# A fixed list of some 1,280 steps laid out anew on five engines and the DMA queue

## The chip, the cores and the metric

The program runs on one core of a Trainium2 chip. A core has five engines, each with an instruction list of its own that it works off in order: TensorE (PE in the profile; PEld is its weight load), VectorE (DVE), ScalarE (ACT), GpSimd (POOL) and SyncE (SP), which here only issues transfers. Engines wait for each other through semaphores. The metric is the device time of one execution in microseconds; lower is better.

## The reference, cut to what matters

```python
# q, k, v: (4, 8, 768, 64); chunks of 32 keys, 24 of them
k_min, k_max = min and max of k over each chunk
ub = sum over d of maximum(q * k_min, q * k_max)       # (B, H, S, 24)
ub = where(causal, ub, -1e9)
top_chunks = the 6 chunks with the largest ub, for each query
scores = matmul(q, k.T) / 8, kept where the chunk is selected and causal
attn = softmax(scores)
x = matmul(attn, v), heads side by side               # (3072, 512)
h = x @ moe_w_in                                      # (3072, 2048)
g = maximum(h, 0) + log1p(exp(-abs(h)))               # softplus
return g @ moe_w_out                                  # (3072, 512)
```

## The kernel before

Attention and feed-forward run side by side. Two heads of one batch make a pair, 16 pairs in all. The pairs of batch 0 are split into halves of the sequence (units 0 to 3 and 4 to 7, three tiles of 128 rows each); the pairs of batches 1, 2 and 3 are whole units (8 to 11, 12 to 15, 16 to 19, six tiles). All that any engine does is one list, the string `ORDER` (line 21 on), worked off at build time: each word is a step, and each step puts its instructions at the end of the lists of its engines. So the order of the words is the order on every engine and in SP's queue, and nothing is reordered at run time: what stands behind a waiting instruction on its engine waits too. A last letter V, A or G names the engine of a copy (VectorE, ScalarE, GpSimd). A tile from a pool waits until an earlier tile's last reader is done; the PSUM pools `ps_big`, `ps_sm` and `ps_w` have two buffers each, the float loads three per kind.

The steps, with unit u, head e, batch b, half h:

- `bk`, `bq`, `bv` (line 211): loads of batch 0, 128 KB each, three to a tile; `hk`, `hq`, `hv` (218, 221, 226): their casts to bf16. `Lk`, `Lq`, `Lv` (232): loads of a whole pair, 384 KB; `ck`, `cq`, `cv` (247, 250): their casts; `fk`, `fq` (267): their transposes by DMA. `w0` to `w3` (501, 504): the two weights, 1 MB each step, issued by GpSimd.
- `kt`, `qt` (276, 283): transposes on TensorE (units 0 to 7). `rg` (290): max or min of K over each chunk; `pk` (295): packs them; `kr`, `qr` (299, 303): K and Q into the operand tiles `Kaug`, `Qaug`; `ar` (203): constant rows of Kaug. `qp`, `qn` (311, 316): positive and negative part of Q; `qp` is a max with 0 on VectorE, or a Relu activation on ScalarE.
- `U` (326, 327): the bounds; `Ua`, `M`, `T` (333, 340, 348 and 349): causal mask, the eight largest, and the selection as rows to be added to Q. These rows reach `Qaug` through TensorE and a copy in units 0 to 7 (`a`, `ac`: 357, 362) and 8 to 11 (`s`, `sc`: 368, 372). In units 12 to 19 `cr` (253) casts Q into one of two row buffers `selqs`, `T` writes its rows beside it, and the flip `fs` (258), a DMA transpose on SP for each head, brings both into `Qaug`. `cr` of unit u + 2 writes the buffer of unit u again.
- `S` (407): scores, in three groups a head; `E` (413): exp; `D` (418): the mask of the diagonal blocks, on GpSimd; `V` (434): times values; `n` (444 to 450): normalisation; `X`, `x` (456, 466) or the DMA transpose `fx` (263): into `xT`.
- `I` (476): four matmuls of the first feed-forward product; `P` (480): softplus; `F` (488): two matmuls of the second; `ob` (492): its copy out of PSUM; `O` (496): the store. `tE` and `tP` (181) change ScalarE's table between exp and softplus.

An `I` block of a batch's half needs all four of its pairs; `F` steps fill TensorE between the `S` and `V` of the next batch.

Of the kernel before, what the change touches and what calls it, by code (L numbers as in the profile page):

```python
# [27 lines left out]
bq1.1.0 hv0.0.0.G U2 qn3 bq1.1.1 E0.0.0 a1.0 hv0.0.1.G Ua2 ac1.0.V a1.1 bq1.1.2 D0.1 M2 S1.0.0 bv1.0.0 D0.0 ac1.1.V
V0.1 E1.0.0 T2 bv1.0.1 U3 S1.1.0 Ua3 bv1.0.2 V0.0 D1.0 M3 E1.1.0 a2.0 bv1.1.0 n0 bv1.1.1 D1.1 ac2.0.V a2.1 bv1.1.2 T3
S2.0.0 Lk8 ac2.1.V a3.0 E2.0.0 a3.1 Lq8 ac3.0.V ac3.1.V V1.0 Lv8 D2.0 V1.1 S2.1.0 n1 S3.0.0 E2.1.0 V2.0 X0 E3.0.0  # L30
S3.1.0 D2.1 x0.A V2.1 D3.0 E3.1.0 n2 X1 hk1.0.A x1.V D3.1 X2 V3.0 V3.1 x2.A Lk9 kt4 n3 kt5 z0 kr4.1.A kr4.0.A rg5.0 X3
# [532 lines left out]
```

## Time and profile before

| | |
|---|---|
| median of 3 runs | 275.47 us (274.07 to 276.18) |
| profiled execution, first to last instruction | 271.8 us |
| TensorE busy | 246.8 us (91%) |
| ScalarE busy | 180.2 us (66%) |
| VectorE busy | 123.0 us (45%) |
| GpSimd busy | 109.5 us (40%) |
| feed-forward matmuls, `F` and `I` | 94.8 and 91.8 us |
| scores, `S` | 52.4 us |

The profile shows one execution. Busy shares are means over the whole span; which wait ends last in a stage is read from that stage. The times of the table of runs and the span of the profiled execution differ by 3.7 us.

### The profile page before, as it was taken

To read this page: it belongs to the slowest core of one execution; us is meant where nothing else is said; L and a number is where in the kernel's file an instruction comes from. 1 tells how busy PE (TensorE), PEld (TensorE's weight loads), DVE (VectorE), ACT (ScalarE), POOL (GpSimd) and SP (SyncE) were. 2 spreads that over 40 slices of the span, in tenths; PEclk is the share of its full clock that TensorE was granted. 3 is DMA by queue.
4 is the path that set the end of the run, shared out by engine and by line. 5 is a ranking of instruction groups with operands and counts; after the bars stand their busy time and mean duration, and the time that the engine had idled before them with its cause. 6 is when DMAs were issued, how large, how long until landed. Compare 5 with 4: busy or idle time off the path is not lost.

```text
span 271.8 us, 5937 instructions
## 1 busy us (share of the span) xinstructions
PE 246.8 (91%) x2295; PEld 153.4 (56%) x2328; DVE 123.0 (45%) x451; ACT 180.2 (66%) x240; POOL 109.5 (40%) x177
## 2 busy tenths in 40 slices
...
GB/s 154 222 195 219 212 169 194 189 151 247 191 233 246 199 189 199 224 160 238 198 151 237 167 177 169 136 128 8 31 2 39 70 68 42 39 0 41 77 77 77
DMA packets 119900, 39.19 MB, mean 144 GB/s; under 512 B 113728, under 2 KB 115776, under 8 KB 119872
## 3 DMA queue, kind: packets, MB, share of 16 engines
...
q8 instruction: 18, 0.29, 0.4%
q14 instruction: 10, 0.08, 0.1%
...
## 4 chain that ended last, share of the span: by engine, by line
PE 87%; ACT 5%; DMA 2%; issue 2%; DVE 2%; POOL 1%; SPq 1%; ACTq 0%; DVEq 0%; POOLq 0%
PE hp L476 30%; PE op L488 30%; PE sc L407 15%; PE o_ps L434 8%; ACT Kaug L203 2%; ACT Kaug L299 1%; DMA Qaug<-row 1%; DMA kf<-in_k_dram 1%; PE ub L326 1%; PE ub L327 1%; PE x_ps L456 1%; PE qa L357 1%; ACT attnT L413 1%; ACT kbh L218 1%; PE sT L368 1%
## 5 line engine op out<-in xcount | busy, mean ns | idle before, releaser
L488 PE MATMUL op<-w_out_sb,gT 128*128 128x512 bf16 x351 | 94.8, 382 | 1.5
L413 ACT ACTIVATE attnT<-sc 128x1024 bf16<-128x1024 f32 (+3 forms) x96 | 82.9, 916 | 16.1 <-PE sc L407 15.4
L476 PE MATMUL hp<-xT,w_in_sb 128*128 128x384 bf16 x512 | 91.8, 326 | 0.2
L480 ACT ACTIVATE gT<-hp 128x768 bf16<-128x768 f32 x64 | 49.2, 808 | 47.1 <-PE hp L476 47.0
L476 PEld LDWEIGHTS <-w_in_sb 128*128 128x128 bf16 x512 | 49.6, 98 | 37.2 <-issue 0.5
L407 PE MATMUL sc<-Qaug,Kaug 128*128 128x128 bf16 (+3 forms) x400 | 52.4, 263 | 1.4 <-ACT attnT L413 0.7
L418 POOL TENSOR_SCALAR_AFFINE_SELECT attnT<-attnT 128x768 bf16<-128x768 bf16 (+1 forms) x40 | 29.2, 731 | 57.3 <-ACT attnT L413 56.9
L488 PEld LDWEIGHTS <-gT 128*128 128x128 bf16 x384 | 35.3, 98 | 28.5 <-issue 0.4
L407 PEld LDWEIGHTS <-Kaug 128*128 128x128 bf16 x400 | 30.6, 101 | 20.8 <-issue 3.0
L434 PEld LDWEIGHTS <-attnT 128*128 128x128 bf16 x672 | 25.3, 98 | 3.2 <-POOL attnT L418 0.3
L434 PE MATMUL o_ps<-vaug,attnT 128*128 128x65 bf16 x672 | 26.7, 194 | 0.3 <-DVE Qaug L362 0.2
L492 ACT COPY ob<-op 128x512 f32<-128x512 f32 x21 | 12.3, 584 | 20.9 <-PE op L488 16.9
L299 POOL COPY Kaug<-kT_sb 64x768 bf16<-64x768 bf16 x24 | 20.2, 841 | 13.1 <-issue 7.0
L290 DVE TENSOR_REDUCE km<-kT_sb 128x24 bf16<-128x768 bf16 x24 | 21.9, 941 | 1.8 <-DMA kT_sb<-kb 1.8
L295 POOL COPY kmm<-km 64x48 bf16<-64x48 bf16 (+1 forms) x40 | 10.4, 259 | 15.9 <-DVE km L290 13.8
L340 DVE MAX8 m<-ubm 128x8 f32<-128x8 f32 (+4 forms) x192 | 16.3, 159 | 0.4
L181 ACT ACT_TABLE_LOAD x11 | 14.1, 1283 | 1.0 <-PEq L548 0.8
L333 DVE TENSOR_TENSOR ubm<-ub,causal 128x288 f32<-128x288 f32 (+2 forms) x20 | 7.5, 379 | 14.8 <-PE ub L327 14.8
L450 DVE TENSOR_TENSOR on<-o_ps,rr 128x384 bf16<-128x384 f32 x24 | 13.4, 557 | 0.8
L492 DVE COPY ob<-op 128x512 f32<-128x512 f32 x3 | 2.0, 682 | 24.0 <-PE op L488 24.0
L449 DVE RECIPROCAL rr<-o_ps 128x6 f32<-128x6 f32 x24 | 4.6, 192 | 18.3 <-PE o_ps L434 18.0
L247 POOL CAST kb<-kf 128x768 bf16<-128x768 f32 x12 | 11.2, 930 | 3.4 <-DMA kf<-in_k_dram 3.3
...
## 6 DMA issues: line engine op xcount, KB each, us to landing
...
w_in_sb<-in_moe_w_in_dram POOLq DMA_DIRECT2D x2, 1024.0 KB, 12.9
...
```

The lines of the kernel that those rows point to most:

```text
L181: A.activation(dummy, dummy, fn)
L290: V.tensor_reduce(st["km2"][:, which, :], st["kT"].rearrange("d (c t g) -> d c t g", t=4, g=CH // 4), axis=AX.XY, op=(ALU.max, ALU.min)[wh ...
L299: COPY[eng](Ka(p, e)[D * (1 - e):D * (2 - e), t0 * 128:t1 * 128], st["kT"][e * D:(e + 1) * D, :])
L340: V.max(out=st["m8"][:, t, e, :], in_=st["ubm"][:, t, 0:max(8, 4 * (t0 + t + 1)), e])
L407: PE.matmul(sc[:, o:o + (z - a) * 128], Ka(p, e)[:, tj * 128:(tj + 1) * 128], Qa(p, e)[:, a * 128:z * 128], start=True, stop=True)
L413: A.activation(st["at", e][:, g * 1024:g * 1024 + n], st["sc", e, g][:, 0:n], ACT.Exp, scale=scale)
L418: G.affine_select(out=d, in_=d, compare_op=ALU.is_ge, fill=0.0, base=0, channel_multiplier=-1, pattern=[[0, n], [1, 128]])
L434: PE.matmul(o[:, t, :], st["at", e][:, a:a + 128], va[:, tj, e, :], start=(tj == 0), stop=(tj == t0 + t))
L476: PE.matmul(hps[b, h, s][:, n, 0:HALF], w_in_sb[:, dt, ft * 128:(ft + 1) * 128], xT[b][:, dt, h * HALF:(h + 1) * HALF], start=(dt == 0), s ...
L480: A.activation(gT[b, h][:, 2 * s:2 * s + 2, :], hps.pop((b, h, s))[:, :, 0:HALF], ACT.Softplus)
L488: PE.matmul(held[b, t], g[:, ft, c:c + 128], w_out_sb[:, ft, :], start=(ft == 0), stop=(ft == KFF - 1))
L492: COPY[eng](obs[b, t], held.pop((b, t)))
```

## The change

`ORDER` is replaced. It holds the same steps (one `tE`, the last of the old list, is gone), in another order, and 130 of the steps that may run on several engines run on another one. Two conditions are changed so that the first step of a tile, whichever it is, allocates it. The list is 81 lines long; shown are the beginning of both and the lines with the steps of units 12 to 19 that are spoken of below.

```diff
@@ -19,81 +19,81 @@
-bk0.0.0 bk0.0.1 augb ident bk0.0.2 cau0 bq0.0.0 kmm bq0.0.1 bq0.0.2 augm rm0.V bk0.1.0 hk0.0.A bk0.1.1 vones rm1.V
-ar1.0.A bk0.1.2 kt0 cau1 kt1 bq0.1.0 rg0.1 ar1.1.A rg0.0 bq0.1.1 kr1.0.A hq0.0.G bq0.1.2 kr0.0.A rg1.0 bv0.0.0 kr0.1.A
-pk0.0.G rg1.1 bv0.0.1 pk0.1.G ar2.0.A qt0 pk1.1.G bv0.0.2 qp0.V pk1.0.G hk0.1.A qn0 bv0.1.0 qt1 U0 kr1.1.A bv0.1.1
-qp1.V ar2.1.A Ua0 kt2 hq0.1.G bv0.1.2 qn1 M0 kt3 kr2.0.A bk1.0.0 U1 rg3.0 kr2.1.A bk1.0.1 ar3.0.A T0 bk1.0.2 rg2.0 w1
-a0.1 kr3.1.A bq1.0.0 rg2.1 kr3.0.A w0 bq1.0.1 Ua1 qt2 ar3.1.A ac0.1.V a0.0 rg3.1 bq1.0.2 pk2.1.G ar0.1.A qp2.V bk1.1.0
-qt3 pk2.0.G ac0.0.V hv0.1.1.G qp3.V bk1.1.1 ar0.0.A S0.1.0 M1 hv0.1.0.G bk1.1.2 pk3.0.G qn2 E0.1.0 S0.0.0 pk3.1.G T1
...
-Lq16 fs13.0 F0.5.7 pk14.0.G I1.1.7.1 cq15.V ob0.5.A pk14.1.G fq15 I1.1.0.0 P1.1.7 Lv16 I1.1.0.1 Lk17 qn14 qp14.V
...
-I1.0.0.0 P1.0.2 F1.3.0 cr14.V I1.0.1.0 Lq17 I1.0.0.1 fs14.0 I1.0.1.1 P1.0.0 fs14.1 rg15.1 kr15.0.G F1.3.1 P1.0.1
-I1.0.4.0 kr15.1.G rg15.0 F1.3.2 I1.0.4.1 pk15.0.G cq16.V pk15.1.G I1.0.3.0 P1.0.4 fq16 F1.3.3 cr15.V Lv17 I1.0.3.1
...
-ck17.G I1.0.5.1 fs15.0 P1.0.7 F1.5.0 fk17 P1.0.5 F1.3.5 Lq18 F1.5.1 rg16.1 tE S13.0.2 S12.1.2 F1.3.6 rg16.0 F1.5.2
...
-cr17.V E13.0.1 O1.3 S12.1.0 D12.0 F1.0.1 qn16 E12.1.0 S12.0.1 qp16.V F1.0.2 E12.0.1 D12.1 S12.0.2 U16 F1.0.3 E12.0.2
...
-E13.1.2 D13.0 fk18 F1.0.5 E13.1.1 F1.5.5 Lq19 cr16.V cv17.G S13.1.0 fx12 V13.0 E13.1.0 rg17.0 fs16.0 kr17.1.G S15.1.2
...
+cau0 bk0.0.0 augb bk0.0.1 bk0.0.2 rm1.V augm ar1.0.G ar3.1.A hk0.0.V bq0.0.0 ident vones bq0.0.2 ar0.0.A bk0.1.1
+bq0.0.1 bk0.1.2 kt1 rg1.1 kmm kt0 kr1.0.A kr1.1.A kr0.0.A rm0.G ar0.1.G ar2.1.A bk0.1.0 bq0.1.1 bq0.1.0 hq0.0.G rg0.0
+rg1.0 pk1.1.A hk0.1.G rg0.1 kr0.1.V bv0.0.1 bk1.0.2 qt0 pk0.0.A bq0.1.2 hq0.1.G qt1 pk0.1.V qp0.A qn0 qn1 ar1.1.A U0
+qp1.A kt2 Ua0 M0 pk1.0.A ar2.0.A T0 rg2.1 bk1.0.0 U1 rg2.0 kt3 a0.1 Ua1 kr2.0.V pk2.1.G kr2.1.A pk2.0.A ac0.1.A
+kr3.1.V M1 a0.0 qt2 bk1.1.0 bv0.0.2 bk1.0.1 qn2 qp2.A S0.1.0 ac0.0.A T1 rg3.0 rg3.1 bq1.0.0 bv0.1.2 bv0.0.0 E0.1.0
+bq1.1.1 bv0.1.0 bq1.0.2 U2 qt3 ar3.0.G a1.0 bq1.0.1 Ua2 qn3 kr3.0.V hk1.0.A bv0.1.1 a1.1 qp3.A M2 pk3.0.V S0.0.0
+ac1.1.V ac1.0.V hv0.0.0.A E0.0.0 kt4 kt5 pk3.1.V T2 kr5.1.A U3 z0 D0.1 kr5.0.V hv0.0.1.G Ua3 rg5.1 z1 w0 S1.1.0 rg5.0
+hq1.0.V kr4.0.V M3 cau1 rg4.1 a2.0 a2.1 S1.0.0 kr4.1.A ac2.0.A E1.1.0 D0.0 bk1.1.1 bk1.1.2 pk5.1.V V0.1 T3 ac2.1.V
+V0.0 n0 w1 D1.1 S2.0.0 E1.0.0 a3.0 ac3.0.V X0 qt4 a3.1 S2.1.0 E2.0.0 x0.V D1.0 V1.1 hv0.1.0.V rg4.0 pk4.0.V ac3.1.A
+D2.0 S3.0.0 V2.0 qt5 V1.0 hv0.1.1.V qp5.V n1 E2.1.0 E3.0.0 D2.1 S3.1.0 V2.1 E3.1.0 qn4 D3.0 X1 pk4.1.V pk5.0.G hk1.1.A
+x1.A n2 D3.1 qp4.V qn5 V3.0 V3.1 X2 n3 kt6 x2.V X3 kt7 x3.V U4 I0.0.3.1 I0.0.3.0 Ua4 I0.0.2.0 rg7.0 bq1.1.0 rg6.1 M4
+bq1.1.2 Lk9 w2 rg6.0 U5 tP P0.0.3 I0.0.2.1 T4 kr6.0.V I0.0.0.0 Ua5 bv1.0.2 bv1.0.0 bv1.0.1 rg7.1 P0.0.2 kr6.1.A
+I0.0.0.1 a4.0 pk6.1.G a4.1 I0.0.1.1 I0.0.1.0 P0.0.0 bv1.1.1 kr7.0.A I0.0.4.1 pk7.0.V I0.0.4.0 hq1.1.V P0.0.1 P0.0.4
+I0.0.7.1 I0.0.7.0 I0.0.6.0 ck9.G qt6 kr7.1.V I0.0.6.1 qt7 M5 ac4.1.A bv1.1.0 bv1.1.2 pk6.0.A P0.0.7 qp6.A T5 I0.0.5.0
+qn6 P0.0.6 ac4.0.A U6 I0.0.5.1 a5.1 qp7.A Ua6 S4.1.1 M6 ac5.1.V a5.0 pk7.1.A qn7 P0.0.5 T6 ac5.0.V U7 tE E4.1.1 S4.1.0
+a6.1 E4.1.0 fk9 Lk8 Ua7 a6.0 ac6.1.V ac6.0.V w3 F0.2.0 F0.1.0 D4.1 M7 F0.2.1 T7 S5.1.0 F0.1.1 S5.1.1 E5.1.0 E5.1.1
+F0.1.2 S4.0.1 a7.1 D5.1 a7.0 E4.0.1 hv1.0.1.V ac7.1.V S4.0.0 V5.1 S5.0.1 E4.0.0 ac7.0.V D4.0 E5.0.1 hv1.0.0.V V4.1
+S5.0.0 F0.2.2 S6.0.1 V4.0 E5.0.0 S6.0.0 F0.2.3 E6.0.1 D5.0 S6.1.0 V5.0 hv1.1.0.V n4 E6.0.0 hv1.1.1.G X4 S6.1.1 D6.0
...
+I1.0.7.1 pk14.0.V I1.0.7.0 I1.1.6.0 kr13.0.A fk15 fq15 Ua13 M13 Lv12 T13 fs13.0 fs13.1 U12 qp14.V Ua12 rg15.1 M12
...
+P1.0.3 I1.1.5.1 I1.1.5.0 F1.3.1 S13.1.0 F1.3.2 P1.1.5 qn15 T12 ck16.V fs12.1 tE E13.1.0 Ua14 cr15.V F1.0.1 F1.3.3
+F1.0.2 S12.1.0 F1.0.3 fs12.0 Lq16 D13.1 fk16 E12.1.0 S13.1.1 F1.0.4 F1.3.4 S12.0.0 E13.1.1 F1.3.5 rg15.0 F1.0.5
...
+F1.5.5 S15.1.0 E14.0.1 cv14.G ck19.G ob1.2.V E15.1.0 F1.5.6 n13.0 T16 cr16.G pk17.1.V kr16.1.V Lk18 cr17.G Lv15 O1.3
+fx12 V14.1 fs16.1 S15.0.1 U17 S15.1.1 Ua17 E15.0.1 F1.5.7 F1.4.0 S15.0.2 M17 T17 E15.1.1 E15.0.2 F1.4.1 ob1.5.V V14.0
+S15.0.0 F1.4.2 fs17.1 fs16.0 S15.1.2 cv15.A D15.1 E15.0.0 kr17.0.G F1.4.3 E15.1.2 F1.1.0 n14.0 S16.1.1 fk19 E16.1.1
+n14.1 S16.1.0 E16.1.0 V15.1 F1.4.4 S17.1.0 E17.1.0 Lv17 F1.1.1 D15.0 ck18.V rg19.0 S17.1.2 rg19.1 F1.1.2 V15.0 fx14
...
+I2.1.3.1 I2.1.3.0 O1.5 I2.0.2.1 P2.1.3 D16.1 kr18.0.G O1.2 I2.0.2.0 P2.0.2 ob1.1.A U18 Ua18 M18 D17.0 T18 F2.0.0
...
+S17.0.1 tE E17.0.1 V16.1 F2.2.0 fs18.1 fs18.0 F2.0.3 S18.1.0 F2.0.4 T19 E18.1.0 kr19.1.V kr19.0.V F2.2.1 fs19.0 F2.0.5
...
+S19.0.0 S18.0.0 V18.1 E18.0.0 ob2.0.V E19.0.0 O2.0 fs19.1 F2.1.0 F2.2.6 S18.0.1 F2.1.1 O1.4 E18.0.1 D19.0 n18.1 F2.2.7
...
@@ -204,7 +204,7 @@
     def load0(c, h, g, t):
-        if t == 0:
+        if (c, h, g) not in quad:
@@ -469,7 +469,7 @@
-        if n == 0:
+        if (b, h, s) not in hps:
```

## Rows read from the trace of the kernel before

**Rows 1.** Table of stages, its sum line: us, busy us of each engine

```profile
sum 271.80, PE 246.81 PEld 153.38 DVE 123.00 ACT 180.25 POOL 109.51; mean PE 17.63 PEld 10.96 DVE 8.79 ACT 12.88 POOL 7.82
```

**Rows 2.** Table of stages: stage, busy us of each engine (instructions), granted clock, DMA, GB/s

```profile
27.75:41.48 13.73, 12.90 (x112) 8.15 (x110) 7.29 (x26) 11.01 (x19) 6.97 (x16) 1.00 1.06 190
...
41.48:61.95 20.47, 18.91 (x257) 13.45 (x258) 11.60 (x49) 17.83 (x22) 11.99 (x16) 1.00 1.08 180
...
136.95:150.00 13.05, 8.12 (x108) 5.60 (x108) 6.37 (x25) 5.42 (x7) 5.32 (x7) 0.74 1.07 192
```

**Rows 3.** TensorE in order of time, 26 to 32 us: start, us, work

```profile
27.75 3.00 PE L476 MATMUL hp<-xT,w_in_sb 128*128 128x384 bf16 x16
```

**Rows 4.** Chain that ended last, 128 to 152 us: start, us, what

```profile
137.74 2.90 DMA Qaug<-row
...
141.89 0.22 PE ub L326
```

**Rows 5.** Waits of TensorE and of VectorE: total us, times, longest

```profile
PE ub L326 <- DVE qpos L311: 4.9, 1, 4.9
...
DVE row L253 <- DMA Qaug<-row: 9.0, 1, 9.0
```

**Rows 6.** The same table in steps of 5 us, 140 to 150 us

```profile
140.00:145.00 5.00, 3.11 (x20) 1.57 (x21) 3.10 (x18) 0.71 (x1) 0.62 (x1) 0.50 0.98 184
145.00:150.00 5.00, 4.95 (x88) 4.03 (x88) 3.27 (x7) 3.65 (x5) 4.22 (x6) 0.91 1.21 233
```

**Rows 7.** The same table, from K's landing to the first `I` step

```profile
4.60:27.75 23.15, 15.28 (x178) 11.26 (x179) 16.04 (x70) 19.69 (x31) 12.36 (x27) 1.00 1.13 213
```

**Rows 8.** Groups of instructions by shape: busy us, mean ns, idle us ahead

```profile
L290 DVE TENSOR_REDUCE km<-kT 128x12 bf16<-128x384 bf16 x16 | 8.5, 553 | 4.9 <-PE kT L276 2.2 <-issue 1.8 <-ACT Kaug L299 0.8
...
L362 DVE COPY Qaug<-qa 128x384 bf16<-128x384 bf16 x16 | 5.3, 350 | 0.8 <-PE qa L357 0.6
...
L253 DVE CAST row<-qf 128x768 bf16<-128x768 f32 x6 | 4.9, 818 | 9.1 <-DMA Qaug<-row 9.0
...
L311 DVE TENSOR_SCALAR qpos<-qT 128x384 bf16<-128x384 bf16 x8 | 2.7, 354 | 2.9 <-PE qT L283 2.8
...
L311 DVE TENSOR_SCALAR qpos<-qT_sb 128x768 bf16<-128x768 bf16 x12 | 4.5, 377 | 0.0
...
L299 ACT COPY Kaug<-kT 64x384 bf16<-64x384 bf16 x16 | 7.4, 472 | 0.3
...
L218 ACT CAST kbh<-kf 128x768 bf16<-128x768 f32 x4 | 3.3, 832 | 2.4 <-DMA kf<-in_k_dram 2.4
...
L181 ACT ACT_TABLE_LOAD x11 | 14.1, 1283 | 1.0 <-PEq L548 0.8
```

**Rows 9.** Chain that ended last, 54 to 65 us: transposes, `F`, `I`

```profile
54.55 0.17 PE x_ps L456 x3
...
59.62 1.29 PE op L488 x6
...
61.95 2.60 PE hp L476 x16
```

**Rows 10.** VectorE in order of time, 142 to 145 us: unit 16

```profile
142.59 0.46 DVE L333 TENSOR_TENSOR ubm<-ub,causal 128x288 f32<-128x288 f32 x1 [0.76 <-PE ub L327]
...
144.20 0.45 DVE L349 TENSOR_TENSOR row<-ubm,m 128x288 bf16<-128x288 f32 x1
```

**Rows 11.** Flips to Qaug, issue to landing, 100 to 183 us

```profile
DMA to landing us min/median/max: 2.7/4.2/7.0
```

**Rows 12.** Issue to landing: loads of 128 KB (L211), then transfers to w_in_sb

```profile
DMA to landing us min/median/max: 2.4/3.5/15.3
...
DMA to landing us min/median/max: 10.4/12.9/15.3
```

**Rows 13.** GpSimd in order of time, 10 to 15 us

```profile
11.21 1.66 POOL L501 DMA_DIRECT2D w_in_sb<-in_moe_w_in_dram  x2
...
14.11 0.95 POOL L226 CAST vaug<-vf 128x384 bf16<-128x384 f32 x2 [0.29 <-DMA vf<-in_v_dram]
```

More of the change, by code (lines that the diff above doesn't have):

```diff
@@ L27 @@
-qt3 pk2.0.G ac0.0.V hv0.1.1.G qp3.V bk1.1.1 ar0.0.A S0.1.0 M1 hv0.1.0.G bk1.1.2 pk3.0.G qn2 E0.1.0 S0.0.0 pk3.1.G T1
[L28 to L31, printed above, removed]
```

106 lines of the change are left out of this document (47 added, 59 removed).

## The prediction

> **What bounds the kernel now.** I read a table of the stages first. Its sum: 271.8 us from first to last instruction, TensorE busy for 246.8 of them [rows 1]. The median of the timed runs is 275.47 us; I make the sum against the profiled 271.8 us and carry the difference, 3.7 us, over unchanged. So all that another order of the same steps can win is some 25 us of idle time and what a low clock costs, none of the matmul work itself. The stages show where TensorE idles [rows 2]. Up to 27.75 us there is no feed-forward work; the first `I` step starts there [rows 3]. Up to 61.95 us TensorE is then idle for 0.83 and 1.56 us (stage length less its busy time). From there it is hardly ever idle, except in the stage 136.95 to 150.00: 13.05 us with 8.12 busy, 4.9 us idle.
>
> That one hole I followed with the chain of waits [rows 4] and the wait tables [rows 5]. TensorE stood at `U16` for 4.9 us, because `qp16` was late on VectorE; VectorE had stood for 9.0 us before `cr16.V`, a cast into one of the two row buffers that units 12 to 19 use in turn, which the flips `fs14` still read; the last of them landed at 140.64 us. So an early cast, waiting in VectorE's list for a transfer late in SP's list, held all behind it. The hole has a second cost: behind it the granted clock is 0.50 for 140 to 145 us and 0.91 for the next five [rows 6], that is 1.2 GHz instead of 2.4. 3.11 us of busy time at half speed lose 1.55 us, 4.95 at 0.91 lose 0.45: 2.0 us. The hole is worth 4.9 + 2.0 = 6.9 us.
>
> **The change, part by part.** No step comes or goes but one spare table load after the last `P`, hidden under closing `F` steps. 130 steps have another engine: GpSimd's lettered steps go from 113 to 57, VectorE's from 67 to 105, ScalarE's from 58 to 76.
>
> *The hole: minus 6.9.* `cr16` goes to GpSimd. Of its six `cr` (14 to 19) VectorE keeps one, `cr15`, and takes `cr12`, which has no flip ahead of it. `cr15` must wait for the flips `fs13`, but `S13.1.0`, which needs them too, stands ahead of it in the list. Behind `cr16` on GpSimd now stand `cr17` and the masks `D15` and `D17`, for which `V15` and `V17` on TensorE would wait; I cost that at nothing, as `fs14.0` stands some 7 us of TensorE's work ahead of `cr16`, and at the old 4.9 us if that cover goes. SP has less ahead of the flips: before `fs13.0` its list holds 23 pair loads, 16 other flips and 4 stores, where it held 26, 18 and 5.
>
> *The start: plus 1.9.* Here VectorE carries more. In 4.60 to 27.75 us it was busy for 16.04 us [rows 7]. Before the first `I` the new list adds four `rg` of units 4 and 5 at 0.553, six `kr` at about 0.35, two `qp` and two `qn` at 0.354, the cast `hq1.0` at up to 0.818, `hk0.0` at up to the same, two `hv` of half its size at 0.4, six `pk` of a sixteenth of its elements at 0.1 (my estimate), two `x` at 0.35: 2.2 + 2.1 + 1.4 + 0.8 + 0.8 + 0.8 + 0.6 + 0.7 = 9.4. It gives away four `qp` and four `ac` at 0.35: 2.8 [rows 8]. (`kr` and `x` go by the copy of L362, the nearest row.) So 16.04 + 9.4 - 2.8 = 22.6 us of work for VectorE. It starts once K is loaded, at about 5 us as before: with no wait the first `I` would start at 27.6 us; with VectorE idle for as long as before, 23.15 - 16.04 = 7.1 us, at 34.7. I take 30.5, nearer to the first: an engine with a longer list waits less, and each wait that work now fills is no loss. Of the 2.75 us by which that is later than 27.75, 0.85 is no loss: `kt6`, `kt7`, `qt4`, `qt5` and `U4` are done by then, 0.17 us each, by three transposes of such a step [rows 9]. Net plus 1.9, ends minus 1.0 and plus 6.1. Behind each of these steps on VectorE stand `Ua`, `M`, `T` of the next unit, and TensorE's `a` steps wait for those.
>
> *Behind the start: minus 1.4.* In 27.75 to 61.95 us 2.4 us are idle [rows 2]; the `kt` and `qt` steps of units 4 to 7, on which TensorE waited there, now lie ahead of the first `I` or behind most of the block. One change of ScalarE's table, 1.28 us [rows 8], stays; I leave 1.0. Ends 0 and minus 2.4.
>
> *The late units: plus 2.0.* This is what the new order pays. I counted TensorE's work between `U` and the first `S` of units 12 to 19 (`I` 0.65, `F` 0.43 a step [rows 9]; `V` and `S` likewise). Before it was 14.7 to 37.8 us; after it is 6.6 (unit 17), 7.1 (18), 7.6 (19), 8.2 (12), 9.6 (16) and 12.9 to 15.2 for the rest. In that time VectorE makes `Ua`, `M`, `T`, 142.59 to 144.65, 2.1 us when nothing is queued ahead [rows 10], and the flip lands 4.2 us after its issue in the median, 2.7 to 7.0 [rows 11]. So 6.3 us are needed, 9.1 at worst. With the median nothing waits; with the worst, 2.5 + 2.0 + 1.5 + 0.9 = 6.9 us. Behind a late flip all of TensorE's list waits, and on SP the second head's flip and the `fx`. I take 2.0, nearer to the median since fewer transfers are ahead; ends 0 and 6.9.
>
> *The relus: 0.* Ten `qp` go to ScalarE. On VectorE they cost 0.354 (units 0 to 7) and 0.377; the nearest rows of ScalarE, copies and casts of such length, take 0.472 and 0.832 [rows 8], so 6 x 0.12 + 4 x 0.46 = 2.6 us more. ScalarE's other work in between gets shorter by six `ob`, six `kr` and two `x`, and TensorE's `I` and `S` cover the rest. Without that cover it is 2.6. The Trainium skill, "ScalarE: Activation LUTs", section "Rules for kernel authors", speaks against this move: relu belongs on VectorE, which it calls up to about three times as fast in bf16. The rows agree on the price (0.377 against 0.832); by that rule the sum would be 273.7, which is rival 5.
>
> *The rest: 0.* In 61.95 to 129.60 and after 150.00 the order keeps TensorE fed with `F` between `S` and `V`; the stores move back in SP's list, each still ahead of the copy that needs its buffer; the tail, copy and store, is the same.
>
> Sum: 271.8 - 6.9 + 1.9 - 1.4 + 2.0 = 267.4; carried to the median, 275.5 - 4.4 = **271.1 us**.
>
> **The rivals.**
> 1. *The start eats the gain* (no change). 128 KB loads landed 3.5 us after issue in the median, but up to 15.3 while the two weight transfers ran, which themselves took 12.9 [rows 12]. Those were issued at 11.21; now they stand behind `hv0.0.1` and `z1` on GpSimd. 18 loads had landed by 14.1 [rows 13], some 0.6 us each, so the 25th, the last that `hq1.0.V` needs, lands at about 18 to 19, just when I expect `w0` to start. If `w0` wins, `hq1.0` holds VectorE, and behind it `M3`, `T3`, `n0` to `n3` and so the first `I`. At the upper end of the start, plus 6.1, it gives 271.1 + 4.2 = 275.3. Against it: those loads are all issued before `w0`.
> 2. *The short chains break* (slower). Place: `S12.1.0` and `S17.1.0`. Landing at 7.0 everywhere costs 6.9 where I took 2.0: 276.0. It decides from the point where one wait is long enough for the clock to fall, as the 4.9 us one did: a flip held on SP by a step that is itself late. One such hole of 6.9 us on top gives 282.9. For it: SP runs in order, and landing already varied from 2.7 to 7.0. Against it: fewer loads ahead.
> 3. *Relu needs its own table* (slower). Each load is 1.28 us, two for each `qp` on ScalarE: 20 x 1.28 = 25.7, of which the first four lie on the start: plus 10.2, 281.3 or more. Against it: 11 loads stand in the trace for 11 deliberate switches [rows 8], and copies run under either table with none. The same skill page, section "Table sets: the hidden batching unit", has relu in every set as filler; by that rule this rival falls, but no relu has run here.
> 4. *Nothing is lost at the start or in the chains*: 271.1 - 2.0 - 2.9 = 266.2, if VectorE never waits and every flip lands in the median.
> 5. *The relus lie on the path*: the first four stand ahead of `U0` to `U3` with nothing to cover them, the others in `I` blocks. All ten uncovered: 271.1 + 2.6 = 273.7.
>
> **How the numbers follow.** About 1% is what a measurement of this kernel can tell from no change: 272.7 to 278.2 us are the same. My forecast, with waits between 0 and 3.5 us, covers 267 to 272.7: 0.48. Rival 4 has 0.07, both faster: 0.55. Rival 1 (0.13), rival 2 without a hole (0.08) and rival 5 (0.04) end within 1%: 0.25. Rival 2 with a hole, 0.16, and rival 3, 0.04, are slower: 0.20. The range leaves out the holes beyond 279, rival 3 and a little below 266.5; the likeliest case's own is 267 to 272.7.
>
> **What would show it.** Right: no wait of VectorE on `Qaug<-row` above 2 us, TensorE's clock at full from 100 to 175 us, the first `I` at 29 to 32 us, each of `S12`, `S15`, `S17` waiting under 1.5 us for a flip. Wrong: a first `I` after 33, `hq1.0` waiting on its load for more than 4 us, a clock of 0.5 in any stretch, or table loads above ten.

## The result, and the profile after

The changed kernel takes 276.8 us (median of 20 runs, 275.6 to 278.5), the kernel before 274.0 us on the same chips (20 runs, 272.3 to 276.7). The ratio is 1.010, 95% interval 1.0078 to 1.0122: 1.0% slower. Forecast were 271.1 us and a gain.

The profiled execution of after has a span of 276.8 us and is the longest of its twenty (273.9 to 276.8). In the runs of both kernels the time is the span plus some 1.7 us; the 3.7 us that the prediction carried over were these 1.7 and another 2.0, since its median came of three runs (275.47, where twenty give 274.0) and the profiled execution of before was a short one (271.8 + 1.7 = 273.5). What follows compares the two profiled spans, 276.8 and 271.8; the medians lie 2.8 us apart, not 5.0.

The busy times on the page of after stand against [rows 1]: engine, busy us, share, instructions. VectorE went up by 20.8 us, GpSimd down by 26.5.

```profile
PE 247.8 (90%) x2295; PEld 155.3 (56%) x2328; DVE 143.8 (52%) x489; ACT 188.1 (68%) x256; POOL 83.0 (30%) x121
```

The table of stages in steps of 10 us, first of after, then of before: stage, length, busy us of TensorE, its weight loads, VectorE, ScalarE, GpSimd (instructions), granted clock, DMA share, GB/s.

```profile
20.00:30.00 10.00, 6.55 (x77) 5.94 (x76) 7.20 (x26) 5.17 (x9) 4.62 (x9) 0.67 1.16 202
30.00:40.00 10.00, 8.16 (x80) 5.39 (x78) 8.28 (x30) 5.80 (x9) 3.96 (x8) 0.82 1.18 207
...
90.00:100.00 10.00, 7.94 (x101) 4.99 (x100) 9.81 (x27) 8.12 (x12) 8.13 (x10) 1.00 0.96 173
100.00:110.00 10.00, 9.02 (x127) 6.78 (x130) 9.09 (x20) 7.66 (x9) 4.50 (x5) 1.00 0.75 168
...
140.00:150.00 10.00, 9.95 (x110) 6.18 (x110) 5.86 (x18) 8.81 (x11) 5.14 (x7) 1.00 0.81 166
150.00:160.00 10.00, 8.94 (x105) 5.62 (x106) 8.23 (x28) 7.82 (x11) 5.78 (x8) 1.00 1.13 212
160.00:170.00 10.00, 8.20 (x120) 5.62 (x118) 8.27 (x29) 7.12 (x9) 4.12 (x5) 1.00 0.79 159
```

```profile
90.00:100.00 10.00, 9.89 (x160) 7.75 (x160) 8.99 (x29) 9.47 (x12) 9.70 (x13) 1.00 1.25 187
...
130.00:140.00 10.00, 6.96 (x46) 3.62 (x44) 1.52 (x3) 7.99 (x11) 2.46 (x4) 0.95 1.02 177
140.00:150.00 10.00, 8.06 (x106) 5.60 (x108) 6.37 (x25) 4.35 (x5) 4.84 (x6) 0.71 1.09 209
```

From tables over the whole span comes the account of the two executions. Idle is stage length less TensorE's busy time, from the table above. Slow clock is an estimate: busy time times what the granted clock lacks of 1.00, from the same table in steps of 1 us, since the clock changes within the stages.

| us | idle before | idle after | slow clock before | after |
|---|---|---|---|---|
| 0 to 40 | 13.3 | 17.0 | 0 | 4.4 |
| 40 to 80 | 1.8 | 0.4 | 0 | 0 |
| 80 to 120 | 0.4 | 3.9 | 0 | 0 |
| 120 to 150 | 5.0 | 0.2 | 2.0 | 0 |
| 150 to 180 | 0.3 | 3.2 | 0 | 0 |
| 180 to the end | 4.2 | 4.2 | 0 | 0 |
| sum | 25.0 | 29.0 | 2.0 | 4.4 |

(Each figure is rounded by itself.) So the hole of [rows 2, 4] and its slow clock are gone: 6.8 us. The start took up to 8.1 back, 80 to 120 us 3.5, 150 to 180 us 3.0; 40 to 80 us gave another 1.4. That makes 6.4 us where the spans differ by 5.0, so the slow clock is put too high. The table in steps of 5 us shows why, first of after, then of new_start_only, an experiment below with the same start:

```profile
25.00:30.00 5.00, 4.90 (x56) 4.59 (x54) 3.14 (x9) 3.64 (x6) 2.06 (x4) 0.50 1.12 203
```

```profile
25.00:30.00 5.00, 4.90 (x57) 4.59 (x55) 3.17 (x9) 3.64 (x6) 2.07 (x4) 1.00 1.12 203
```

In after the clock was at its lower level, 1.2 GHz, and TensorE got through the same work in these 5 us; the first `I` comes at 34.68 us, in new_start_only at 34.21. So up to there the slow clock cost some 0.5 us, as far as one execution of each can say, and the 4.4 is an upper end.

Where TensorE waits now, and one wait of ScalarE (waits of after, as in [rows 5]: engine, line, releaser, us in all, times, longest):

```profile
PE kT L276 <- DVE kbh L218: 6.2, 1, 6.2
PE qT L283 <- DVE km L290: 3.0, 1, 3.0
PE o_ps L434 <- DVE Qaug L362: 2.9, 1, 2.9
PE ub L326 <- DVE kmm L295: 2.2, 2, 1.7
PE ub L326 <- DVE qpos L311: 1.5, 1, 1.5
PE sT L368 <- DVE on L450: 1.3, 1, 1.3
...
PE sc L407 <- DMA Qaug<-row: 0.9, 1, 0.9
...
ACT Kaug L299 <- DVE km L290: 5.7, 2, 3.4
```

Of the waits of TensorE shown here all but one end with VectorE. The first, 6.2 us, is for K's landing and cast. Behind it the longest at the start are 3.0 us before the first `qt` and 2.9 before `V0.1`. The PSUM buffer of `V0.1` is that of `a2.1`, and the copy that frees it, `ac2.1.V`, stands in VectorE's list behind `rg` of units 4 and 5, the cast `hq1.0`, `kr4.0` and `M3`, `T3` (VectorE and TensorE of after in order of time):

```profile
20.84 1.01 DVE L290 TENSOR_REDUCE km<-kT 128x12 bf16<-128x384 bf16 x2
21.77 0.55 DVE L221 CAST row<-qf 128x768 bf16<-128x768 f32 x1
...
24.14 0.35 DVE L362 COPY Qaug<-qa 128x384 bf16<-128x384 bf16 x1
...
24.55 0.82 PE L434 MATMUL o_ps<-vaug,attnT 128*128 128x65 bf16 x12 [2.91 <-DVE Qaug L362]
...
34.68 3.27 PE L476 MATMUL hp<-xT,w_in_sb 128*128 128x384 bf16 x12
```

In 85 to 101 us GpSimd holds VectorE up for part of the time. A copy of 64x48 elements to `kmm`, 0.19 us elsewhere, lasts from 92.23 to 93.88, as long as the memset `zs0` of GpSimd beside it, and `U11` waits. Added up over all of VectorE's instructions, the time above the shortest of the same form is 17.6 us in after, 8.8 in before; records of instructions overlap, so less than that was lost. The rows of the moment (the same view, VectorE, GpSimd and TensorE):

```profile
92.23 1.65 DVE L295 COPY kmm<-km 64x48 bf16<-64x48 bf16 x1
...
92.24 1.59 POOL L512 MEMSET row<- 128x1792 bf16 x1
...
94.98 0.20 PE L326 MATMUL ub<-kmm,qpos 128*128 128x48 bf16 x1 [1.49 <-DVE qpos L311]
```

### The profile page after: what moved, and what is told of

It is laid out like the page before. It is cut to its first block, busy times and chain, and to the rows that moved or that the text cites. A ratio compares the mean times of both kernels' runs of the same rounds, so it can differ in the third digit from the quotient of the medians.

```text
span 276.8 us, 5895 instructions
## 1 busy us (share of the span) xinstructions
PE 247.8 (90%) x2295; PEld 155.3 (56%) x2328; DVE 143.8 (52%) x489; ACT 188.1 (68%) x256; POOL 83.0 (30%) x121
## 4 chain that ended last, share of the span: by engine, by line
PE 73%; DVE 10%; SPq 5%; ACT 5%; DMA 4%; issue 2%; ACTq 0%
PE hp L476 29%; PE op L488 24%; PE sc L407 10%; PE o_ps L434 6%; SPq L211 4%; DVE m L340 2%; DMA Qaug<-row 1%; DMA xT<-on 1%; ACT attnT L413 1%; DMA vf<-in_v_dram 1%; PE x_ps L456 1%; ACT L181 1%; DVE kmm L295 1%; DVE km L290 1%; DVE ubm L333 1%
## 5 line engine op out<-in xcount | busy, mean ns | idle before, releaser
L488 PE MATMUL op<-w_out_sb,gT 128*128 128x512 bf16 x351 | 93.2, 379 | 1.5
L476 PE MATMUL hp<-xT,w_in_sb 128*128 128x384 bf16 x512 | 90.4, 329 | 0.3 <-DMA xT<-on 0.3
L480 ACT ACTIVATE gT<-hp 128x768 bf16<-128x768 f32 x64 | 51.9, 810 | 31.4 <-PE hp L476 31.3
L407 PE MATMUL sc<-Qaug,Kaug 128*128 128x128 bf16 (+3 forms) x400 | 53.5, 262 | 2.2 <-DMA Qaug<-row 0.9
L492 DVE COPY ob<-op 128x512 f32<-128x512 f32 x9 | 6.2, 689 | 54.2 <-PE op L488 54.1
L492 ACT COPY ob<-op 128x512 f32<-128x512 f32 x15 | 8.6, 583 | 21.6 <-PE op L488 21.6
L299 POOL COPY Kaug<-kT_sb 64x768 bf16<-64x768 bf16 x12 | 10.4, 868 | 9.5 <-DMA kT_sb<-kb 9.0
L247 DVE CAST qb<-qf 128x768 bf16<-128x768 f32 x4 | 5.7, 1425 | 11.5 <-DMA qf<-in_q_dram 11.5
L326 PE MATMUL ub<-kmm,qpos 128*128 128x48 bf16 (+1 forms) x96 | 7.9, 185 | 4.2 <-DVE kmm L295 2.2
L290 DVE TENSOR_REDUCE km<-kT 128x12 bf16<-128x384 bf16 x16 | 8.3, 548 | 1.9 <-ACT Kaug L299 1.3
```

The lines of the kernel that those rows point to most:

```text
L290: V.tensor_reduce(st["km2"][:, which, :], st["kT"].rearrange("d (c t g) -> d c t g", t=4, g=CH // 4), axis=AX.XY, op=(ALU.max, ALU.min)[wh ...
L407: PE.matmul(sc[:, o:o + (z - a) * 128], Ka(p, e)[:, tj * 128:(tj + 1) * 128], Qa(p, e)[:, a * 128:z * 128], start=True, stop=True)
L476: PE.matmul(hps[b, h, s][:, n, 0:HALF], w_in_sb[:, dt, ft * 128:(ft + 1) * 128], xT[b][:, dt, h * HALF:(h + 1) * HALF], start=(dt == 0), s ...
L480: A.activation(gT[b, h][:, 2 * s:2 * s + 2, :], hps.pop((b, h, s))[:, :, 0:HALF], ACT.Softplus)
L488: PE.matmul(held[b, t], g[:, ft, c:c + 128], w_out_sb[:, ft, :], start=(ft == 0), stop=(ft == KFF - 1))
L492: COPY[eng](obs[b, t], held.pop((b, t)))
```

## The experiments

Each ratio is to the kernel before, runs taken on the same chip. The diffs give the steps moved; where a kernel's own line numbers are one higher than those here, that is its longer list of steps.

| kernel | us | ratio, 95% interval |
|---|---|---|
| after | 276.8 | 1.0100 (1.0078 to 1.0122) |
| one_cast | 268.5 | 0.9795 (0.9738 to 0.9851) |
| new_order_old_engines | 280.9 | 1.0222 (1.0191 to 1.0253) |
| old_order_new_engines | 284.4 | 1.0356 (1.0324 to 1.0388) |
| old_start_new_rest | 280.4 | 1.0209 (1.0156 to 1.0262) |
| new_start_only | 274.9 | 1.0019 (0.9973 to 1.0065) |
| old_to_45 | 285.3 | 1.0341 (1.0264 to 1.0418) |
| old_to_45_b | 275.4 | 1.0054 (1.0010 to 1.0098) |
| new_mid_only | 281.7 | 1.0272 (1.0211 to 1.0332) |
| old_to_115 | 270.2 | 0.9826 (0.9783 to 0.9869) |
| early_ac2 | 277.4 | 1.0089 (1.0046 to 1.0132) |
| units45_later | 280.5 | 1.0235 (1.0168 to 1.0301) |
| early_zs0 | 275.9 | 1.0047 (1.0004 to 1.0090) |
| mid_moves | 274.6 | 1.0005 (0.9965 to 1.0045) |
| three_moves | 275.3 | 1.0056 (1.0020 to 1.0093) |
| four_moves | 273.9 | 0.9989 (0.9957 to 1.0020) |
| qp_vector | 278.8 | 1.0171 (1.0102 to 1.0240) |

**The hole alone: one_cast.** Read again, the trace of before names another cast than the prediction did (VectorE in order of time):

```profile
131.22 0.56 DVE L247 CAST qb<-qf 128x768 bf16<-128x768 f32 x1 [0.26 <-DMA qf<-in_q_dram]
140.74 0.56 DVE L253 CAST row<-qf 128x768 bf16<-128x768 f32 x1 [8.95 <-DMA Qaug<-row]
...
148.06 1.09 DVE L253 CAST row<-qf 128x768 bf16<-128x768 f32 x1
```

In the list `cr17.V` stands between `cq17.V` (131.22) and `qp16`; `cr16.V` stands behind `T16` and is the one at 148.06. The cast that waited is `cr17`, and the flips are `fs15`.

```
-cq17.V ... cr17.V E13.0.1 ... qn16 ... qp16.V ... qn17 ... qp17.V
+cq17.V ... E13.0.1 ... qn16 ... qp16.V ... qn17 ... qp17.V cr17.V
```

> The kernel before with one step moved: the cast cr17.V stands behind qp17.V and no longer ahead of qn16 and qp16. (The trace of before, read again, shows that the cast that held VectorE for 9.0 us was cr17 waiting for the flips fs15, not cr16 as the prediction has it.) Theory of the hole: the idle 4.9 us of TensorE at U16 and the slow clock behind it go, 6.9 us less, 274.0 - 6.9 = 267.1 us. Rival, the wait only moves: T16 or the flips of unit 16 stand late all the same, less than 2 us gained, 272 us or more.

268.5 us, 2.0% under before (6.1 us by the medians of this chip, 274.6). `U16` no longer waits, and the clock is full to the end of TensorE's work. The price of the hole was right, under a wrong name. This is the lowest median of the study, by one step moved; only old_to_115, which has the same cure, comes as low within the intervals.

**Order and engines crossed.**

```
new_order_old_engines:  each step of the new list with the letter of the old one (130 letters)
old_order_new_engines:  the list of one_cast, each step with the letter of the new one
```

> The new order of steps, each step on the engine that it had before. Theory E (the copies given to VectorE and ScalarE cost the time: VectorE carries too much up to the first I and in 85 to 105 us): VectorE's busy time falls back from 143.8 to about 123 us, the first I comes at 31 us or sooner instead of 34.7, the idle 2.1 us of TensorE in 90 to 100 us shrinks under 1 us, and the time is 271 us or less. Theory O (the order itself costs it: steps stand in the list ahead of what they could have done): as late as after, 276 us or more, since GpSimd's copies take 0.8 to 0.9 us where VectorE's take 0.35 to 0.6.

> The order of the first of these runs (that of before, with cr17 behind qp17), each step on the engine that the change gives it. Theory E: VectorE is late at the start here too, first I after 30 us instead of 27.75, and the time is 3 us or more above that of the first run, 270 us or more if that one is at 267. Theory O: the engines matter little, within 1.5 us of the first run.

| | old engines | new engines |
|---|---|---|
| old order (cr17 behind qp17) | 268.5 | 284.4 |
| new order | 280.9 | 276.8 |

Neither theory holds by itself. The new engines cost 16 us in the old order and save 4 in the new one. With new order and old engines VectorE is back at 123.1 us busy, and TensorE waits for GpSimd instead: 4.1 us in all before `U` for its copies to `kmm`. With old order and new engines VectorE is busy 9.8 of 10 us in 90 to 100 and in 110 to 120. Each list is fitted to its own engines.

One sign of theory E failed in new_order_old_engines. The first `I` should have come at 31 us or sooner with VectorE relieved; it came at 35.15, later than in after (the stretch from K's landing to the first `I`, then TensorE in order of time):

```profile
4.60:35.15 30.55, 18.69 (x196) 14.96 (x197) 19.55 (x82) 21.20 (x34) 15.57 (x34) 0.99 1.22 214
```

```profile
35.15 1.13 PE L477 MATMUL hp<-xT,w_in_sb 128*128 128x384 bf16 x3
```

VectorE is busy for 19.55 us there and idle for 11.0. With old order and new engines the first `I` comes at 30.90. So the late first `I` goes with the new order, on either set of engines. Behind the start it is alike: in 80 to 120 us and in 150 to 180 us new_order_old_engines has 3.9 and 3.1 us of idle time, after has 3.9 and 3.2.

**Stages exchanged.** The list up to a seam from the one kernel, then what is left of the other's.

```
old_start_new_rest:  before, up to ahead of its first I        | after
old_to_45:           before, 268 steps (end of the I block)    | after
old_to_45_b:         the same, loads of units 8 and 9 not in it | after
new_start_only:      after, up to the same point               | one_cast
new_mid_only:        as old_to_45_b up to 115 us               | one_cast
old_to_115:          one_cast, 648 steps                       | after
```

> All steps that stand ahead of the first I in the kernel before, in their old order and on their old engines, then what is left of the changed kernel in its own order and on its own engines. If the start is what ate the gain (first I at 34.7 instead of 27.75 us, and a granted clock of 0.67 and 0.82 in 20 to 40 us), the first I is back at about 28 us and the time is 276.8 - 6 = 271 us or less. If the loss lies behind the start (idle TensorE in 80 to 110 and 150 to 180 us), the time stays at 275 us or more.

> All that the kernel before does up to the end of its first I block (its first 268 steps, to about 45 us), in the old order and on the old engines, then what is left of the changed kernel in its own way. The seam lies where both lists have done nearly the same steps (it was ahead of the first I in old_start_new_rest, where TensorE then waited 2.6 and 1.4 us for units 4 and 5). Theory S (the start costs the change 3.7 us of idle TensorE up to 40 us and 3.6 us of slow clock, less 1.4 in 40 to 80 us): 276.8 - 5.9 = 271 us. Rival: the start's loss is only handed on, 275 us or more.

> The same with the seam at about 115 us (648 steps), so that only the late units 12 to 19 stand in the new way, and the wait of cr17 is not there. With what the profile shows of the new layout behind 115 us (idle TensorE of 3.0 us in 150 to 180 us that the kernel before does not have), and no wait at U16, 268.5 + 3 = 271.5 us. If the short chains from U over T and the flip to S cost nothing by themselves: 268.5 us. If the loss of 3.5 us in 80 to 110 us is a loss of its own, old_to_45 lies 3 us above this one.

> The new order and engines up to the end of the first I block (about 45 us), then what is left of one_cast (the kernel before with cr17 behind qp17) in its old way. Theory S (the start costs most): 268.5 + 5 to 6 = 274 us. Rival M (the middle and the interplay with it cost most, since early_ac2 won nothing): 268.5 + 0 to 2, 270.5 us or less.

> The old way up to 45 us, the new way from there to about 115 us, the old way again behind it. Idle TensorE in 80 to 110 us was 3.5 us more in the changed kernel than in the one before. Theory of the long VectorE queue: 268.5 + 3.5 = 272 us, with a wait of 1.5 us before U11 and one of 1.3 us before s11. If the middle is harmless once the start is on time: 268.5 to 269.5 us.

> As old_to_45, but with the loads of units 8 and 9 left to the new list (in old_to_45 the load for ck9 stood in SP's list behind one that waited for its buffer, and GpSimd, waiting for it, held back the masks of units 4 to 7: 6.7 us). Theory S: 276.8 - 5 to 6 = 271 to 272 us. Theory M: 275 us or more.

Three of these tell more of seams than of stages. In old_start_new_rest the steps of units 4 and 5 still stood ahead of the first `I`, at 33.45 us. In old_to_45 GpSimd's cast `ck9` waited 14.9 us for a load that SP had behind another; the masks of units 4 to 7 stood behind the cast. In new_mid_only GpSimd waited up to 4.1 us for V loads, with the copies to `kmm` behind them (waits of old_to_45, then of new_mid_only):

```profile
PE o_ps L434 <- POOL attnT L418: 6.7, 1, 6.7
...
POOL kb L247 <- DMA kf<-in_k_dram: 15.5, 2, 14.9
```

```profile
PE ub L327 <- POOL kmm L296: 6.4, 1, 6.4
...
POOL vaug L251 <- DMA vf<-in_v_dram: 7.2, 2, 4.1
```

Both are the mechanism of `cr17` once more, made by accident: a cast that waits for a transfer, in a list that others need, makes TensorE wait 6 to 7 us (4.9 with `cr17`), and the granted clock falls to 0.50 behind it. Without the early load old_to_45_b is 9.9 us below old_to_45.

The clean ones price the stages. The new start alone costs 6.4 us (274.9 less 268.5), the late units alone 1.7 (270.2; by the ratios 0.8, and the intervals overlap, so it may be nothing), middle and late units together 6.9 (275.4). The middle is then some 5 us by the difference; new_mid_only agrees only roughly: its span of 281.0 less 6.4 us of the wait and 4.3 of slow clock (again an upper end) leaves 270.3, 4.2 above that of one_cast. Start and rest add up to 13.3, the whole is 8.3: the parts overlap. Why the new rest is cheaper behind the new start than behind the old one stays open.

**Moves within the changed kernel, at the start.**

```
early_ac2:      ... rg5.0 [a2.0 a2.1 ac2.1.V ac2.0.A] hq1.0.V ... E1.0.0 [kr4.1.A] ...
units45_later:  X3 x3.V I0.0.3.1 [kt4 kt5 rg5 kr5] I0.0.3.0 [hq1.0.V rg4 kr4 pk5 pk4 qt4] tP P0.0.3 ... [U4] I0.0.0.0
```

> The changed kernel with four steps of units 2 and 4 moved. In its trace TensorE waits 2.9 us before V0.1 (21.64 to 24.55 us), whose PSUM buffer is that of a2.1; the copy that frees it, ac2.1.V, stands on VectorE behind rg5.1, rg5.0, hq1.0, kr4.0, M3, rg4.1, pk5.1 and T3, and ac2.0.A on ScalarE behind kr4.1.A, which waits 3.4 us for rg4.1. Here a2.0, a2.1, ac2.1.V and ac2.0.A stand ahead of hq1.0.V, and kr4.1.A behind E1.0.0. Theory L (work for later units stands in the list ahead of what TensorE needs now, and the slow clock in 20 to 40 us follows from that wait): the wait before V0.1 is under 0.7 us, the granted clock is full in 20 to 40 us, and the time is 276.8 - 2.2 - 3.6 = 271 us. Rival W (VectorE has too much work up to the first I, in whatever order): the wait turns up at the next steps, first I still after 33 us, 275 us or more.

> The changed kernel with the steps of units 4 and 5 that stand ahead of its first I (kt, rg, kr, pk, qt, qp, qn, hq1.0 and U4, and kt6, kt7) put behind it, in between the first I steps. Theory S with its cause in the order: VectorE is through with units 0 to 3 sooner, the first I comes at 29 to 31 us instead of 34.7, and the time is 3 us or more lower, 273.5 or less. If units 4 and 5 only come late in their turn: first I at 30 us but a wait before U5, a4 or S4 instead, and the time within 1 us of 276.8.

early_ac2: the wait before `V0.1` is gone and of the slow clock 1.6 us are left, but the time is the same (277.4) and the first `I` comes at 33.27 us. The next `a` step waits 2.3 us for VectorE's `T` instead, and `S15` 2.9 us for its flip. units45_later: the first `I` comes at 29.11 us, as foreseen, and the time rises to 280.5; `qt4` and the mask rows now wait for VectorE in the `I` block (TensorE in order of time):

```profile
33.13 0.44 PE L283 MATMUL qT<-ident,row 128*128 128x128 bf16 x3 [2.10 <-DVE row L221]
...
39.87 0.34 PE L357 MATMUL qa<-ident,row 128*128 128x128 bf16 x3 [0.96 <-DVE row L349]
```

So early_ac2 went as its rival W said: the wait only moves. units45_later went as its second case said, with waits in the `I` block instead, but came out higher than either case had it (273.5 or less, or within 1 us of 276.8). VectorE has more to do up to the first `I`, as a single stretch of the table of stages shows, from K's landing to the first `I` of after, against [rows 7]:

```profile
4.60:34.68 30.08, 17.68 (x197) 14.22 (x198) 23.25 (x91) 19.66 (x36) 15.38 (x30) 0.87 1.19 216
```

VectorE is busy for 23.25 us and idle for 6.8; before it was 16.04 and 7.1. But its work alone does not set the pace: new_order_old_engines has 19.55 us of it and the same late first `I`. Most of the delay comes with the new order, which puts the steps of units 4 and 5 among those of units 0 to 3; with most of these moved behind, the first `I` came 5.6 us sooner. Which chain of waits holds it to some 35 us on either set of engines, and why moving these steps wins nothing in the whole time, stays open.

**Moves within the changed kernel, in the middle.**

```
early_zs0:    ... kr8.0.G [zs0] ...                 (from ahead of F0.0.7)
mid_moves:    early_zs0, and ... n9.1 [ck13.V] ...  (from ahead of M11)
three_moves:  early_ac2, early_zs0, and pk17.0.A [pk17.1.V] (from behind T16)
four_moves:   three_moves and ck13.V as in mid_moves
```

> The changed kernel with one GpSimd memset moved: zs0 (1.59 us) stands behind kr8.0.G, at about 68 us, where VectorE has little to do, no longer at 92.24 to 93.83 us, where a VectorE copy of 64x48 elements to kmm, 0.19 us elsewhere, takes 1.65 us and ends when the memset ends. Theory C (a VectorE instruction on SBUF stands still while a GpSimd instruction uses the memory): the copy takes 0.2 us or waits for the next GpSimd instruction in its place, TensorE's 1.5 us before U11 falls under 0.6 us, and the time is 1.5 to 2.5 us lower, 274.3 to 275.3 us. Rival (the long copy is a matter of how the record is kept, or of the copy's own work): the copy is still 1.6 us long and the time stays within 0.5 us.

> The changed kernel with zs0 early, as in early_zs0, and the cast ck13.V (1.07 us) behind n9.1, ahead of which it stood when TensorE waited 1.3 us for n9.1 before s11. If VectorE's queue up to n9.1 is what TensorE waits for in 85 to 101 us, that wait falls under 0.5 us and the time is 1 us below early_zs0, 274.5 to 275 us. If VectorE has no slack there, the wait turns up behind the next steps (S10, X8) and the time stays at early_zs0's 275.9 us.

> Both of these moves in one, and the copy pk17.1.V of unit 17 to kmm ahead of kr16.0.V, ob1.2.V, n13.0 and T16 on VectorE, behind which it stood when TensorE waited 1.75 us for it before U17. If each loss is its own and they add up: 276.8 - 5.8 - 2.0 - 1.7 = 267.3 us. If VectorE is simply full in 85 to 105 us and up to the first I, what one move gains shows up as another wait: 272 us or more.

> The changed kernel with the moves of three_moves and of mid_moves together. If the losses add up: mid_moves stood at 274.6 us, three_moves 1.5 us below after; so 273 to 273.5 us, under the kernel before. If the start is bound by VectorE's work and not by those positions, the moves at the start win nothing and the time stays at that of mid_moves, 274.5 us. Both leave 4 us or more to one_cast (268.5 us).

With the memset at 66.55 us the same copy takes 0.18 us and `U11` does not wait (VectorE, then TensorE of early_zs0):

```profile
90.39 0.18 DVE L295 COPY kmm<-km 64x48 bf16<-64x48 bf16 x1
...
91.60 0.20 PE L326 MATMUL ub<-kmm,qpos 128*128 128x48 bf16 x1
```

0.9 us are won by the medians (1.5 by the ratios), where 1.5 to 2.5 were foreseen; the intervals of early_zs0 and after overlap a little, so this time by itself is not clear of noise. With `ck13` moved as well 2.2 us are won (2.6), as foreseen and clear of it. In mid_moves TensorE is idle for 0.4 us in 90 to 110, where after has 3.0 (table of stages of mid_moves):

```profile
90.00:100.00 10.00, 9.57 (x142) 6.72 (x140) 9.04 (x31) 9.01 (x12) 7.27 (x9) 1.00 0.85 141
100.00:110.00 10.00, 10.00 (x147) 7.01 (x146) 8.10 (x17) 7.12 (x9) 2.07 (x3) 1.00 1.17 206
```

three_moves, 275.3 us, is not told from early_zs0 (275.9): had the losses added up, it would have been at 267.3. four_moves, 273.9 us, is not told from mid_moves (274.6) nor from before. The moves at the start win nothing, again.

**The relus: qp_vector.** All ten `qp` back on VectorE.

```
-qp0.A qp1.A qp2.A qp3.A qp6.A qp7.A qp13.A qp15.A qp17.A qp19.A
+qp0.V qp1.V qp2.V qp3.V qp6.V qp7.V qp13.V qp15.V qp17.V qp19.V
```

> The changed kernel with the ten relus (qp) back on VectorE, as the prediction cost them at nothing (2.6 us without cover). If they lie on no path, within 1 us of 276.8. If the relus on ScalarE cost time (rival 5, and each must wait for the qn of its unit on the other engine), 1 to 3 us lower. If VectorE is the bound where they stand (units 0 to 3 and 11 to 19), 1 to 3 us higher, as 10 instructions of 0.35 us come back to it.

278.8 us, 2 above after; the intervals overlap a little. So the relus on ScalarE cost nothing that these runs can tell, and may have saved up to 2 us: `U17` waits 2.3 us for VectorE here, where after has 1.7.

**VectorE beside GpSimd: beside.** One list of VectorE instructions at the end of one_cast, under four conditions, one execution.

```
+ for k in alone, 8 x memset, 8 x copy, 8 x mask on GpSimd, alone:
+     twice: copy 64x48, copy 64x768, cast 128x288, min 128x768, reduce 128x768, compare 128x288
```

> The kernel one_cast with a list of VectorE instructions added near its end, where VectorE and GpSimd have nothing to do: copy 64x48, copy 64x768, cast 128x288 from float32, min 128x768, reduce 128x768 to 128x24, compare 128x288 of two float32 inputs, each twice; first with GpSimd idle, then beside GpSimd memsets of 128x1792, beside GpSimd copies of 128x768, beside its masks on 128x768, then with GpSimd idle again. Theory C: those forms that were stretched in the traces (copies, casts and min, from SBUF to SBUF, in 16-bit or with a cast) end when the GpSimd instruction beside them ends, so each takes up to 1.6 us beside a memset; reduce and compare keep their time. Rival (it is the memory traffic that slows both): all of them take longer by the same share, under twice their time alone.

VectorE alone (211 to 214 us), beside memsets (216 to 223), beside copies (231 to 234) and beside masks (240 on), then GpSimd, all in order of time:

```profile
211.84 0.16 DVE L525 COPY kmm<-kmm 64x48 bf16<-64x48 bf16 x1
...
212.53 0.35 DVE L528 TENSOR_SCALAR Kaug<-Kaug 128x768 bf16<-128x768 bf16 x1
212.79 0.94 DVE L529 TENSOR_REDUCE Kaug<-Kaug 128x24 bf16<-128x768 bf16 x1
...
216.78 1.45 DVE L525 COPY kmm<-kmm 64x48 bf16<-64x48 bf16 x1
...
220.04 1.82 DVE L528 TENSOR_SCALAR Kaug<-Kaug 128x768 bf16<-128x768 bf16 x1
221.78 0.93 DVE L529 TENSOR_REDUCE Kaug<-Kaug 128x24 bf16<-128x768 bf16 x1
222.64 0.44 DVE L531 TENSOR_TENSOR Kaug<-causal 128x288 bf16<-128x288 f32 x1
...
231.19 0.34 DVE L526 COPY Kaug<-Kaug 64x768 bf16<-64x768 bf16 x1
...
232.31 1.02 DVE L528 TENSOR_SCALAR Kaug<-Kaug 128x768 bf16<-128x768 bf16 x1
...
234.10 1.10 DVE L531 TENSOR_TENSOR Kaug<-causal 128x288 bf16<-128x288 f32 x1
...
240.77 0.85 DVE L527 CAST Kaug<-causal 128x288 bf16<-128x288 f32 x1
241.55 0.34 DVE L528 TENSOR_SCALAR Kaug<-Kaug 128x768 bf16<-128x768 bf16 x1
```

```profile
216.59 13.64 POOL L515 MEMSET row<- 128x1792 bf16 x8
...
230.34 7.42 POOL L517 COPY Kaug<-Kaug 128x768 bf16<-128x768 bf16 x8
```

Beside the memsets copies, casts and min stand still until the memset ends: the same copy takes 0.16 or 1.45 us. Beside copies and masks they do so in part: the cast each time, the copy of 64x48 each second time, the min beside copies but not beside masks, the copy of 64x768 never. The reduction never does; the compare does once in six, beside copies. It goes the other way too: GpSimd's memsets take 1.59 to 1.72 us here, its copies 0.82 to 1.00. So theory C holds with a limit, that it is not always VectorE that waits, and its rival (all slower by the same share) does not hold.

## Why the prediction was wrong

1. *The hole, minus 6.9: right.* The account has 4.8 of idle time and 2.0 of slow clock, 6.8; one_cast alone is 6.1. The names were wrong, as told above, and with them the worry over `cr16` on GpSimd. Had the cast been read off the list at its time, the smallest cure would have been in sight.
2. *The start, plus 1.9: the step that failed.* The working gave two ends, 27.6 us for the first `I` with no waits of VectorE and 34.7 with VectorE idle for as long as before, and I chose 30.5 because "an engine with a longer list waits less, and each wait that work now fills is no loss". That reason failed. The first `I` came at 34.68; the work was 23.25 us where I had 22.6, and the idle time was 6.8 where it had been 7.1, so the longer list waited as much as the shorter one. That the upper end met 34.68 so closely is partly luck. It priced the start by VectorE's work alone, and new_order_old_engines, with 19.55 us of that work, has 11.0 us of idle time and its first `I` at 35.15: the order itself brings it late, which the working did not hold. Two sizes were off as well: six `pk` took 1.8 us where my estimate was 0.6 (one of them, at 18.44, stood 0.89 us beside a memset), and three `rg` came in, not four. The links that I saw in the chain, ScalarE's `kr4.1` behind `rg4.1` and `ac2.1` behind `hq1.0`, are not the cause: early_ac2 undid both and won nothing. Nor did the sum hold a slow clock there, up to 4.4 us in this execution; but new_start_only has its first `I` only 0.5 us sooner without it, and with early_ac2 and three_moves it is 1.6 and 0 and the time hardly falls, so it is not the main part. The trace gives up to 8.1 for the start, new_start_only 6.4; the upper end was 6.1. Which chain sets the pace there stays open.
3. *Behind the start, minus 1.4: right.* Idle time in 40 to 80 us went from 1.8 to 0.4.
4. *The late units, plus 2.0: about right, by another cause.* 3.0 us of idle time in 150 to 180 us; old_to_115 is 1.7 us above one_cast by the medians, which is not clear of noise. Of the 3.0 us 0.9 is a flip (`S15`), which is the wait that I had priced; 1.7 is `U17`, for which VectorE packs K behind `T16`: the queue on VectorE, not the transfers. The size was luck in part. The flips landed in 2.8 us in the median where [rows 11] has 4.2.
5. *The rest, 0: wrong.* 3.5 us in 80 to 120 us, in after on VectorE, busy for 9.81 of 10 us in 90 to 100. I looked at what stood between `S` and `V` on TensorE and not at what the moved copies do to VectorE's queue there. In [rows 1] VectorE has 123 us of 272 and seems free; in this stage it was at 8.99 of 10 even before. It is not VectorE's load alone here either: new_order_old_engines has as much idle time there, with GpSimd busy for 9.5 us and more in each of 90 to 100 and 100 to 110. Two steps moved in the list (mid_moves) bring 3.9 us of idle time in 80 to 120 down to 1.3.
6. *The relus: right* to cost them at nothing, as far as qp_vector can tell.

Of the rivals, 1 named the right place and nearly the price (275.3) with the wrong cause: `hq1.0` did not wait for its load. 2 had its chains but no hole. 3 fell: ten table loads for ten switches, beside ten relus. 4 and 5 did not come. Of the signs put down as right, those on the hole all came (VectorE waits 0.8 us at most for `Qaug<-row`, the clock is full from 100 to 175 us); of those put down as wrong, a first `I` after 33 us and a clock of 0.50 (25 to 30 us).

One kind of loss stood in none of them: VectorE held up by GpSimd, as the copy of 0.16 us that takes 1.45 beside a memset shows. The Trainium skill, "SBUF — State Buffer", section "SBUF: two separate sides", says that VectorE and GpSimd share a pair of memory ports by an exclusive lock: a VectorE instruction in a two-port mode and a GpSimd instruction exclude each other for the whole of either, and one with two SBUF inputs only where GpSimd reads. The trace agrees as to the memsets (copy held, compare not, 0.44), and in the one compare held beside copies (1.10). It has one more compare beside copies and two beside masks that were not held (0.44). The copies and casts between SBUF tiles that the change takes from GpSimd to VectorE are of the kind that is held, and VectorE meets the rest of GpSimd's work with them. What this cost over the whole kernel was not measured apart; early_zs0 prices one such meeting at about 1 us.

On the pair of readers of one PSUM tile: the trace shows ScalarE's copy waiting 3.4 us for VectorE's reduction, though both only read. The Trainium skill, "PSUM — Partial Sum Buffer", section "PSUM bank collisions raise a hardware error", has two engines at one bank as an error, reads included, which would be the reason to order them; no run here shows the error.
